# Five PSUM banks in one ring, output half columns in turns and merged VectorE work, in a fused forward and backward pass of an SSM and a gated FFN

## The chip, the core and the metric

The kernel runs on one core of a Trainium2 chip. A core has a matrix engine (TensorE, PE in the profile; its weight loads are PEld), a vector engine (VectorE, DVE), a scalar engine (ScalarE, ACT), GpSimd (POOL) and the queues that issue DMA (SP and others). Matmul results land in PSUM, which has eight banks; each holds 512 fp32 values per partition. VectorE or ScalarE must copy a result out of its bank before the bank is used again. SBUF is the memory for everything else on the core.

The metric is the device time of one execution, in microseconds (us). Of a kernel several executions are timed, and the median is given.

## The reference, cut to what matters

The input x (2048 rows of 576 columns, bf16) is normalised. The output is x plus a state-space convolution of xn (branch A) plus a gated FFN of xn (branch B). The program computes this output and, for a given grad_out, the gradients of x, of all parameters of A and of the three FFN matrices.

```python
def _B_ref(x, W_gate, W_up, W_down):            # D = 576, F = 4608
    gate = x @ W_gate
    up = x @ W_up
    gate = gate * (gate > 0)
    h = gate * up
    return h @ W_down

def _A_ref(u, A_re, A_im, B_re, B_im, C_re, C_im, log_dt, Dskip):
    dt = exp(log_dt)                            # per column d, N = 128 states
    P = exp(dt * A * l)                         # l = 0 .. 2047
    K = einsum("dn,dnl,dn->dl", C, P, dt * B).real
    y = causal_convolution(u, K)                # by rfft / irfft over 2 * L
    return y + u * Dskip

xn = layernorm(x)
out = x + _A_ref(xn, ...) + _B_ref(xn, ...)
# returned: out and the vjp of grad_out for x, A's eight parameters, W_gate, W_up, W_down
```

## The kernel before: the parts that matter

The FFN goes over the hidden size in 12 chunks (c) of 384 columns, each of three tiles (ft) of 128; the rows go in four segments (sg) of 512. The convolution (class S4) is cut into many small steps, which are interleaved with the FFN's by estimates of time; a scheduler orders the instructions of each engine.

PSUM is divided among three pools. Three banks hold FFN products and outputs, three belong to S4, and two to the FFN's transposes ("turns"):

```python
g.psum_mm = pool("psum_mm", 3, space=PSUM)
g.psum_s4 = pool("psum_s4", 3, space=PSUM)
g.psum_t = pool("psum_t", 2, space=PSUM)
```

A unit of the FFN makes gate, up and dh (the gradient of h) for 128 hidden columns and 512 rows: three groups of five matmuls of 512 columns (line L244). ScalarE applies relu, VectorE makes the masked up (upm), h and the two gradients; turns of earlier units are woven in, of which each is four 128x128 transposes and one copy:

```python
def a_unit(self, c, sg, ft, turns=()):
    ...
    for i, rhs in enumerate((xT, xT, gT)):
        ...
        ps = g.psum_mm.tile([P, 512], F32, name="ps_mm")
        for k in range(NK):
            nc.tensor.matmul(ps[:], lhsT=w[:, k, fs], rhs=rhs[:, k, :], ...)      # L244
        pss.append(ps)
        for _ in turns:
            next(src)
        yield ...
    ps_g, ps_u = pss[0:2]
    ...
    nc.scalar.activation(rg[:], ps_g[:], ACT.Relu)                                # L252
    nc.vector.scalar_tensor_tensor(upm[:], rg[:], 0.0, ps_u[:], op0=ALU.is_gt, op1=ALU.mult)   # L254
    nc.vector.tensor_tensor(hT[:], rg[:], upm[:], op=ALU.mult)                    # L256
    ...
    g.bal.copy(dhb, pss[2][:], 512)
    nc.vector.tensor_tensor(dgT[:], dhb, upm[:], op=ALU.mult)                     # L262
    nc.vector.tensor_tensor(duT[:], dhb, rg[:], op=ALU.mult)                      # L264
```

`bal.copy` gives a copy out of PSUM to VectorE or ScalarE by a running estimate of their loads (lines L62 and L68 in the profile).

An output step makes, for 128 rows, the two outputs (0: the FFN's output from h, three matmuls a group; 1: the gradient of xn from dg and du, six), each in two halves of 288 columns:

```python
def outdx(self, c, sg, j, last=None, turns=()):
    ...
    for which in range(2):
        for hf in range(2):
            ...
            ps = g.psum_mm.tile([P, 512], F32, name="ps_mm")
            for i, (lt, rh, cs) in enumerate(mms):
                nc.tensor.matmul(ps[:, cs], lhsT=lt, rhs=rh, ...)                 # L301
            if last is None:
                g.bal.copy(o[:, which, hs], ps[:, :DH], DH)
            ...
        if which == 0:
            yield FTC * 0.245
    ...
    yield FTC * 0.49
```

Its result is added to an accumulator in DRAM (osx to acc_dram). The last chunk instead adds S4's parts and finishes the outputs.

In S4, the products of two complex spectra (real and imaginary parts stacked on partitions, 96 such products):

```python
def product(self, pool, wpool, A, B, conj):
    ...
    v.tensor_tensor(t[:], A, B, op=ALU.mult)                                      # L666
    for i in range(2):
        r = slice(i * 64, (i + 1) * 64)
        v.tensor_tensor(Z[0:64, i, :], t[r, 0, :], t[r, 1, :], ...)               # L669
    v.tensor_tensor(t[:, 0, :], A[:, 0, :], B[:, 1, :], op=ALU.mult)              # L670
    v.tensor_tensor(t[:, 1, :], A[:, 1, :], B[:, 0, :], op=ALU.mult)              # L671
    for i in range(2):
        r = slice(i * 64, (i + 1) * 64)
        v.tensor_tensor(Z[64:P, i, :], t[r, 1, :], t[r, 0, :], ...)               # L674
    g.bal.add(d=1.6)
```

and, for each of 144 groups of four columns, the powers Y = A0 * B1 + V with V = A1 * B0 (L876 to L878, 1024 bf16 elements each), their use as weights of small matmuls (L903), their transposes (L913), and the sums that the parameter gradients need (matmuls L927):

```python
    for vi, r0 in enumerate((1, 0)):
        pr = gp.tile(sh, F32, name="pr")                                          # one buffer
        nc.vector.tensor_tensor(pr[:], X[...], psg[...], op=ALU.mult)             # L931
        nc.vector.tensor_reduce(out=Sm[:, vi, ...], in_=pr[:], op=ALU.add, axis=AX.X)   # L932
```

Of the kernel before, what the change touches and what calls it, by code (L numbers as in the profile page):

```python
# [10 lines left out]
F32 = mybir.dt.float32  # L11
# [67 lines left out]
def make_consts(g):  # L79
    nc, consts = g.nc, g.consts  # L80
    g.ident_bf = consts.tile([P, P], BF16, name="ident_bf")
    make_identity(nc, g.ident_bf[:])
    g.ident_f = consts.tile([P, P], F32, name="ident_f")
    make_identity(nc, g.ident_f[:])
# [14 lines left out]
def col_store(g, pool, psum, col, dst):  # L99

    nc = g.nc
    ps = psum()
    nc.tensor.transpose(out=ps[:NK, :P], in_=col, identity=g.ident_f[:])
# [14 lines left out]
def ln_group(g, pools, sg, x4, gT):  # L118
# [28 lines left out]
            nc.scalar.activation(x4[:, j, :], x4[:, j, :], ACT.Identity, bias=neg[:, j:j + 1])  # L147
    for j in range(JS):
        nc.vector.tensor_scalar(xn4[:, j, 0:D], x4[:, j, :], g.rinv[:, t0 + j:t0 + j + 1], None, op0=ALU.mult)
        pt = g.psum_t.tile([P, 8, P], BF16, name="pt")  # L150
        for k in range(NK):
            nc.tensor.transpose(out=pt[:, k, :], in_=xn4[:, j, k * P:(k + 1) * P], identity=g.ident_bf[:])
        (nc.vector.tensor_copy if j % 2 == 0 else nc.scalar.copy)(xT[:, :, j * P:(j + 1) * P], pt[:, 0:NK, :])  # L153
# [7 lines left out]
class Ffn:  # L161
# [68 lines left out]
    def a_unit(self, c, sg, ft, turns=()):  # L230

        g, nc = self.g, self.g.nc
        src = self.t_steps(turns)
        xT, gT = self.X[(c, sg)]
        fs = slice(ft * P, (ft + 1) * P)
        pss = []
        dhb = self.dh0.get(ft) if (c, sg) == (0, 0) else None
        for i, rhs in enumerate((xT, xT, gT)):
            if i == 2 and dhb is not None:
                continue  # L240
            w = self.wd[i]
# [9 lines left out]
        rg = self.ep.tile(shp, BF16, name="rg")  # L251
        nc.scalar.activation(rg[:], ps_g[:], ACT.Relu)  # L252
        upm = self.ep.tile(shp, BF16, name="upm")
        nc.vector.scalar_tensor_tensor(upm[:], rg[:], 0.0, ps_u[:], op0=ALU.is_gt, op1=ALU.mult)  # L254
        hT = self.tp.tile(shp, BF16, name="hT")
        nc.vector.tensor_tensor(hT[:], rg[:], upm[:], op=ALU.mult)  # L256
# [4 lines left out]
        dgT = self.tp.tile(shp, BF16, name="dgT")  # L261
        nc.vector.tensor_tensor(dgT[:], dhb, upm[:], op=ALU.mult)  # L262
        duT = self.tp.tile(shp, BF16, name="duT")
        nc.vector.tensor_tensor(duT[:], dhb, rg[:], op=ALU.mult)  # L264
        self.T[(c, sg, ft)] = (hT, dgT, duT)

    def t_steps(self, units):
        g, nc = self.g, self.g.nc
        for c, sg, ft in units:
            for src, dst in zip(self.T[(c, sg, ft)], (self.hN, self.dgN, self.duN)):  # L270
                pt = g.psum_t.tile([P, 8, P], BF16, name="pt")
                for j in range(JS):
                    nc.tensor.transpose(out=pt[:, j, :], in_=src[:, j * P:(j + 1) * P], identity=g.ident_bf[:])  # L273
                g.bal.copy(dst[:, sg * JS:(sg + 1) * JS, ft * P:(ft + 1) * P], pt[:, 0:JS, :], 512, fp32=False)
                yield

    def outdx(self, c, sg, j, last=None, turns=()):
# [7 lines left out]
            last.begin(t)  # L285
        src = self.t_steps(turns)
        Ts = [self.T[(c, sg, ft)] for ft in range(FTC)]
        for which in range(2):
            for hf in range(2):
                hs = slice(hf * DH, (hf + 1) * DH)  # L290
                if which == 0:
                    mms = [(Ts[ft][0], self.wf[:, 0, ft, hs]) for ft in range(FTC)]
# [11 lines left out]
                else:  # L304
                    last.take(t, which, hf, hs, ps[:, :DH])
                next(src, None)
            if which == 0:
                yield FTC * 0.245
        if last is not None:
            last.end(t)  # L310
        elif c == 0:
            nc.gpsimd.dma_start(g.acc_dram[:, t, :, :], o[:])
        else:
            nc.gpsimd.dma_start(g.acc_dram[:, t, :, :], o[:], accum_op=ALU.add)  # L314
        yield FTC * 0.49

    def rows(self, c, i):

# [144 lines left out]
class Ahead:  # L463
# [3 lines left out]
        self.load, self.total, self.n = load, total, n  # L467
        self.next, self.q = 0, {}

    def get(self, i):  # L470
        while self.next < min(i + self.n, self.total):
            self.q[self.next] = self.load(self.next)
            self.next += 1
        return self.q.pop(i)

class S4:
# [183 lines left out]
    def product(self, pool, wpool, A, B, conj):  # L660

        g, nc = self.g, self.g.nc
        t = wpool.tile([P, 2, DH], BF16, name="pr_t")
        Z = pool.tile([P, 2, DH], BF16, name="pr_z")
        v = nc.vector
        v.tensor_tensor(t[:], A, B, op=ALU.mult)  # L666
        for i in range(2):
            r = slice(i * 64, (i + 1) * 64)
            v.tensor_tensor(Z[0:64, i, :], t[r, 0, :], t[r, 1, :], op=ALU.add if conj else ALU.subtract)  # L669
        v.tensor_tensor(t[:, 0, :], A[:, 0, :], B[:, 1, :], op=ALU.mult)  # L670
        v.tensor_tensor(t[:, 1, :], A[:, 1, :], B[:, 0, :], op=ALU.mult)  # L671
        for i in range(2):
            r = slice(i * 64, (i + 1) * 64)
            v.tensor_tensor(Z[64:P, i, :], t[r, 1, :], t[r, 0, :], op=ALU.subtract if conj else ALU.add)  # L674
        g.bal.add(d=1.6)
        return Z


# [120 lines left out]
    def p2_pools(self, c):  # L799
# [2 lines left out]
        lv = cp.tile([P, ST], F32, name="lv")  # L802
        iota(nc, lv[:], [[1, ST]], 0, 16)
        return (lv,) + tuple(self.pool(c, n, bufs) for n, bufs in (
            ("k_par", 1), ("k_dk", 2), ("k_ex", 2), ("k_x", 1), ("k_xo", 2), ("k_uv", 1), ("k_yo", 3), ("k_yt", 2), ("k_g", 1)))

    def p2(self, hf, pools, pw):

        g, nc, bal = self.g, self.g.nc, self.g.bal
        v = nc.vector  # L810
        lv, parp, dkp, exp_, xp, xop, uvp, yop, ytp, gp = pools
        pend, turned = [], []
        Sm = parp.tile([P, 2, DH, 2], F32, name="Sm")

# [3 lines left out]
            return ex  # L818

        def load_dk(i):  # L820
            dkr = dkp.tile([P, ST, SC], BF16, name="dkr")
            nc.sync.dma_start(dkr[:].rearrange("p (q a) d -> p q a d", q=4), self.dk_dram[hf][:, :, i])
            return dkr
        exq, dkq = Ahead(load_ex, DH // SX, 2), Ahead(load_dk, DH // SC, 2)
        for gi in range(DH // SC):
            s0 = gi * SC
            dkr = dkq.get(gi)
# [3 lines left out]
            nc.gpsimd.tensor_tensor(dkc[:, :, 1, :], dkv, lv[:].unsqueeze(1).to_broadcast([P, SC, ST]), op=ALU.mult)  # L831
            Kst = dkp.tile([P, ST, SC], BF16, name="Kst")
            for x0 in range(0, SC, SX):
                hs = slice(hf * DH + s0 + x0, hf * DH + s0 + x0 + SX)
                ex = exq.get((s0 + x0) // SX)
                xs = [P, SX, NE]
# [31 lines left out]
                for dd in range(x0, x0 + SX, DG):  # L868
# [11 lines left out]
                    pend.append((Y, XC, X, dkc, Kst, Sm, s0, dd, dd - x0, hf, gi))  # L880
                    yield 2.1
                    if len(turned) > 0:
                        self.sums(turned.pop(0), gp)
                        yield 0.8
                    if len(pend) > 1:
                        yield from self.turn(pend.pop(0), ytp, turned)
        while pend or turned:
            if turned:
                self.sums(turned.pop(0), gp)
                yield 0.8  # L890
            if pend:
                yield from self.turn(pend.pop(0), ytp, turned)
# [23 lines left out]
        turned.append((YT, X, dkc, Sm, s0, dd, dx))  # L916
        yield 0.4

    def sums(self, item, gp):

        g, nc, bal = self.g, self.g.nc, self.g.bal
        YT, X, dkc, Sm, s0, dd, dx = item
# [5 lines left out]
        sh = [P, DG, 2, 32]  # L928
        for vi, r0 in enumerate((1, 0)):
            pr = gp.tile(sh, F32, name="pr")  # L930
            nc.vector.tensor_tensor(pr[:], X[:, dx:dx + DG, r0:r0 + 2].rearrange("p d r a -> p d (r a)").unsqueeze(2).to_broadcast(sh), psg[:, 0:DG * 64].rearrange("p (d j c) -> p d j c", j=2, c=32), op=ALU.mult)  # L931
            nc.vector.tensor_reduce(out=Sm[:, vi, s0 + dd:s0 + dd + DG, :], in_=pr[:], op=ALU.add, axis=AX.X)  # L932
        bal.add(d=1.3)

    def param_grads(self, hf, Sm, pw, xp, yop):

# [175 lines left out]
def kernel(  # L1112
# [30 lines left out]
    g.out_dskip = out_9  # L1143
    pool = lambda name, bufs, **kw: ctx.enter_context(tc.tile_pool(name=name, bufs=bufs, **kw))
    g.consts = pool("consts", 1)
    g.psum_mm = pool("psum_mm", 3, space=PSUM)
    g.psum_s4 = pool("psum_s4", 3, space=PSUM)
    g.psum_t = pool("psum_t", 2, space=PSUM)
    g.dram = pool("dram", 1, space=DRAM)
    make_consts(g)  # L1150
    d = lambda name, shape, dt=BF16: g.dram.tile(shape, dt, name=name)
# [100 lines left out]
```

## Time and profile before

Three runs of the kernel before took 1817.7 to 1819.48 us, the median is 1818.5 us. The profiled execution spans 1820.2 us.

| Engine | Busy, us | Share of the span | Instructions |
|---|---|---|---|
| PE (matmuls) | 1731.2 | 95% | 16303 |
| PEld (weight loads) | 1186.8 | 65% | 16449 |
| DVE (VectorE) | 1359.8 | 75% | 3181 |
| ACT (ScalarE) | 1184.4 | 65% | 2710 |
| POOL (GpSimd) | 205.0 | 11% | 246 |

A row of instruction groups gives line, engine, operation, result and operands, the shape and the count; then the busy time in us, the mean length of one in ns, and the idle time of the engine just before them with what ended it. For example:

```profile
L68 ACT CAST osx<-ps_mm 128x288 bf16<-128x288 f32 x675 | 262.2, 427 | 74.3 <-PE ps_mm L301 71.4
L254 DVE SCALAR_TENSOR_TENSOR upm<-rg,ps_mm 128x512 bf16<-128x512 bf16 x144 | 98.5, 684 | 92.6 <-PE ps_mm L244 70.7
L932 DVE TENSOR_REDUCE Sm<-pr 128x8 f32<-128x256 f32 x288 | 119.9, 416 | 3.6
```

Copies of output halves on ScalarE take 427 ns each; before them ScalarE stood idle for 74.3 us in all, of which 71.4 us ended when PE finished an output group. A row of waits gives who waited for whom, and then the total in us, how often, and the longest. A row of a timeline gives start and length in us, engine, line and work. The matmuls' ends are modelled, and some matmul records are missing from the trace (2000 of L244's 2145).

### The profile page before, as it was taken

The numbers are of one execution on the slowest core, as the hardware profiler recorded it, in microseconds if no ns is written. First come the engines' busy times: TensorE is split into PE (matmuls) and PEld (weight loads), VectorE is DVE, ScalarE is ACT, GpSimd is POOL, SyncE is SP. The second block draws the span as 40 slices with busy tenths as digits, with TensorE's granted clock in tenths as the row PEclk, the third lists the DMA queues.
The fourth block names the chain that finished last, engine by engine and source line by source line (L and its number), as shares of the span: only waits on it lengthen the run. The fifth ranks groups of instructions, "written<-read, shape, count | busy, mean of one in ns | idle before, by whom it ended". The sixth has DMA issues, their size and how long they took to land. (4 is left out here: it accounts for less than half of the span.)

```text
span 1820.2 us, 42157 instructions
## 1 busy us (share of the span) xinstructions
PE 1731.2 (95%) x16303; PEld 1186.8 (65%) x16449; DVE 1359.8 (75%) x3181; ACT 1184.4 (65%) x2710; POOL 205.0 (11%) x246
## 2 busy tenths in 40 slices
PE   7998998999999999999999999999999999999998
PEld 5664556668566666766756766766676675676776
DVE  7575886676888789669687889989979863983551
ACT  5874774686578478568468657747756845764551
POOL 0200012012012012011101101101111100110000
PEclk9999999999999999999999999999999999999999
DMA  8798999678568676776757856856675578995883
GB/s 288 261 323 307 286 263 292 188 189 231 177 132 199 179 185 136 222 193 153 216 159 175 237 159 136 213 178 159 155 198 137 94 219 248 267 291 152 264 250 96
DMA packets 239004, 373.30 MB, mean 205 GB/s; under 512 B 49490, under 2 KB 153428, under 8 KB 237268
## 3 DMA queue, kind: packets, MB, share of 16 engines
q1 hardware_dynamic: 212836, 304.09, 51.6%
q0 software_dynamic: 24384, 51.92, 18.9%
q10 hardware_dynamic: 1584, 14.60, 2.3%
q8 instruction: 128, 2.10, 0.5%
q14 instruction: 72, 0.59, 0.1%
HBM read 233.10 MB, written 137.43 MB: 204 GB/s over the span
## 5 line engine op out<-in xcount | busy, mean ns | idle before, releaser
L68 ACT CAST osx<-ps_mm 128x288 bf16<-128x288 f32 x675 | 262.2, 427 | 74.3 <-PE ps_mm L301 71.4
L314 POOL DMA_DIRECT2D acc_dram<-osx x160 | 138.5, 866 | 1073.0 <-ACT osx L68 718.8
L301 PE MATMUL ps_mm<-wf,dgT 128*128 128x288 bf16 x1152 | 208.6, 288 | 13.7 <-ACT osx L68 7.7
L355 PEld LDWEIGHTS <-rows 128*128 128x128 bf16 x1536 | 146.1, 98 | 96.7 <-issue 6.9
L301 PE MATMUL ps_mm<-wf,duT 128*128 128x288 bf16 x1152 | 206.9, 288 | 0.0
L301 PE MATMUL ps_mm<-wf,hT 128*128 128x288 bf16 x1152 | 185.2, 288 | 15.3 <-DVE upm L254 9.3
L244 PE MATMUL ps_mm<-gT,wd_160 128*128 128x512 bf16 x694 | 176.3, 381 | 6.3 <-ACT obd L68 4.4
L244 PE MATMUL ps_mm<-xT,wd_159 128*128 128x512 bf16 x711 | 178.4, 379 | 0.6 <-issue 0.2
L244 PE MATMUL ps_mm<-xT,wd_158 128*128 128x512 bf16 x595 | 168.9, 379 | 7.6 <-ACT xT L153 0.7
L254 DVE SCALAR_TENSOR_TENSOR upm<-rg,ps_mm 128x512 bf16<-128x512 bf16 x144 | 98.5, 684 | 92.6 <-PE ps_mm L244 70.7
L339 PE MATMUL ps_mm<-rows,hN 128*128 128x144 bf16 x2304 | 158.4, 226 | 0.0
L339 PEld LDWEIGHTS <-hN 128*128 128x128 bf16 x2304 | 147.4, 98 | 4.1 <-issue 1.4
L68 ACT CAST obw<-ps_mm 128x384 bf16<-128x384 f32 x104 | 49.5, 477 | 147.5 <-PE ps_mm L355 116.1
L301 PEld LDWEIGHTS <-dgT 128*128 128x128 bf16 x1152 | 107.7, 98 | 47.5 <-issue 21.9
L355 PE MATMUL ps_mm<-dgN,rows 128*128 128x384 bf16 x768 | 137.4, 328 | 0.6 <-ACT rg L252 0.6
L355 PE MATMUL ps_mm<-duN,rows 128*128 128x384 bf16 x768 | 136.6, 326 | 0.6 <-DVE upm L254 0.5
L301 PEld LDWEIGHTS <-hT 128*128 128x128 bf16 x1152 | 104.8, 98 | 44.8 <-issue 15.5
L301 PEld LDWEIGHTS <-duT 128*128 128x128 bf16 x1152 | 113.3, 99 | 29.8
L252 ACT ACTIVATE rg<-ps_mm 128x512 bf16<-128x512 f32 x144 | 87.2, 606 | 55.1 <-PE ps_mm L244 52.9
L932 DVE TENSOR_REDUCE Sm<-pr 128x8 f32<-128x256 f32 x288 | 119.9, 416 | 3.6
L68 ACT CAST dhb<-ps_mm 128x512 bf16<-128x512 f32 x141 | 84.0, 595 | 56.9 <-PE ps_mm L244 54.8
L244 PEld LDWEIGHTS <-wd_159 128*128 128x128 bf16 x720 | 65.3, 98 | 61.9 <-issue 1.5
(2517 smaller groups left out, 3534.1 us busy)
## 6 DMA issues: line engine op xcount, KB each, us to landing
acc_dram<-osx POOLq DMA_DIRECT2D x176, 288.0 KB, 4.9
gT<-in_gT_dram SPq DMA_DIRECT2D x48, 640.0 KB, 6.3
xT<-xT_dram SPq DMA_DIRECT2D x44, 640.0 KB, 6.1
rows<-in_gq_dram SPq DMA_DIRECT2D x48, 576.0 KB, 4.6
wf<-in_Wf_dram ACTq DMA_DIRECT2D x11, 1296.0 KB, 9.3
ex_dram<-exs SPq DMA_DIRECT2D x36, 320.0 KB, 4.0
ex<-ex_dram SPq DMA_DIRECT2D x36, 320.0 KB, 4.3
out_dram<-obw SPq DMA_DIRECT2D x96, 96.0 KB, 2.5
```

Source lines behind the costliest of these rows:

```text
L68: self.nc.scalar.copy(out, in_)
L244: nc.tensor.matmul(ps[:], lhsT=w[:, k, fs], rhs=rhs[:, k, :], start=(k == 0), stop=(k == NK - 1))
L252: nc.scalar.activation(rg[:], ps_g[:], ACT.Relu)
L254: nc.vector.scalar_tensor_tensor(upm[:], rg[:], 0.0, ps_u[:], op0=ALU.is_gt, op1=ALU.mult)
L301: nc.tensor.matmul(ps[:, cs], lhsT=lt, rhs=rh, start=(i == 0), stop=(i == len(mms) - 1))
L314: nc.gpsimd.dma_start(g.acc_dram[:, t, :, :], o[:], accum_op=ALU.add)
L339: nc.tensor.matmul(ps[:, ft * 144:(ft + 1) * 144], lhsT=self.hN[:, st, ft * P:(ft + 1) * P], rhs=gq[:, st, :], start=(st == 0), stop=(st = ...
L355: nc.tensor.matmul(ps[:, :Fc], lhsT=xs[:, st, 0:P], rhs=src[:, st, :], start=(st == 0), stop=(st == ST - 1))
L932: nc.vector.tensor_reduce(out=Sm[:, vi, s0 + dd:s0 + dd + DG, :], in_=pr[:], op=ALU.add, axis=AX.X)
```

## The change

It has five parts.

1. The five banks of FFN products and turns become one ring of five.
2. An output step goes through its groups half by half: output 0 and output 1 of the first half, then both of the second, instead of both halves of output 0 first. The points at which S4's steps may come in move along with it.
3. The two FFN gradients are one VectorE instruction over 1024 elements, with dh read twice; h and the gradients lie in one tile.
4. The two products of the sums go into one buffer (that of V) and one reduction takes both. In the products of spectra, the two cross products get a tile of their own (w), the multiplications come first, and the four additions are ordered so that less changes in partitions from one to the next.
5. To make room, the fp32 identity and the pool of pr go, and dkr has one buffer instead of two, loaded ahead in the middle of a group.

It is for letting PE run further ahead of the engines that empty its banks, and for less VectorE work per unit.

```diff
-    g.psum_mm = pool("psum_mm", 3, space=PSUM)
+    g.psum_mm = pool("psum_mm", 5, space=PSUM)
     g.psum_s4 = pool("psum_s4", 3, space=PSUM)
-    g.psum_t = pool("psum_t", 2, space=PSUM)
...
-                pt = g.psum_t.tile([P, 8, P], BF16, name="pt")
+                pt = g.psum_mm.tile([P, 512], F32, name="ps_mm")[:].bitcast(BF16).rearrange("p (k t) -> p k t", t=P)
... (the same for the turns of the normalised input)
-        for which in range(2):
-            for hf in range(2):
+        for hf in range(2):
+            for which in range(2):
...
-            if which == 0:
-                yield FTC * 0.245
+            if hf == 0:
+                yield FTC * 0.3675
...
-        yield FTC * 0.49
+        yield FTC * 0.3675
... (a_unit)
+        ru = self.ep.tile([P, 2, JS * P], BF16, name="rg")
+        upm, rg = ru[:, 0], ru[:, 1]
...
+        T = self.tp.tile([P, 3, JS * P], BF16, name="T")
+        nc.vector.tensor_tensor(T[:, 0], rg, upm, op=ALU.mult)
...
-        nc.vector.tensor_tensor(dgT[:], dhb, upm[:], op=ALU.mult)
-        nc.vector.tensor_tensor(duT[:], dhb, rg[:], op=ALU.mult)
+        nc.vector.tensor_tensor(T[:, 1:3], dhb.unsqueeze(1).to_broadcast([P, 2, JS * P]), ru[:], op=ALU.mult)
... (product)
+        w = wpool.tile([P, 2, DH], BF16, name="pr_w")
         v.tensor_tensor(t[:], A, B, op=ALU.mult)
...
+            v.tensor_tensor(w[:, i, :], A[:, i, :], B[:, 1 - i, :], op=ALU.mult)
+        top, low = slice(0, 64), slice(64, P)
+        re = lambda i, r: v.tensor_tensor(Z[0:64, i, :], t[r, 0, :], t[r, 1, :], ...)
+        im = lambda i, r: v.tensor_tensor(Z[64:P, i, :], w[r, 1, :], w[r, 0, :], ...)
+        re(0, top)
+        im(0, top)
+        im(1, low)
+        re(1, low)
+        g.bal.add(d=2.0)
... (dkr)
-            dkr = dkp.tile([P, ST, SC], BF16, name="dkr")
+            dkr = drp.tile([P, ST, SC], BF16, name="dkr")
...
+                if x0 > 0 and gi + 1 < DH // SC:
+                    dkq.ahead(gi + 1)
... (sums)
+        pr = uvp.tile([P, DG, 2, P], BF16, name="V")[:]. ... .bitcast(F32). ...
         for vi, r0 in enumerate((1, 0)):
-            pr = gp.tile(sh, F32, name="pr")
-            nc.vector.tensor_tensor(pr[:], X[...], psg[...], op=ALU.mult)
-            nc.vector.tensor_reduce(out=Sm[:, vi, ...], in_=pr[:], op=ALU.add, axis=AX.X)
-        bal.add(d=1.3)
+            nc.vector.tensor_tensor(pr[:, vi], X[...], psg[...], op=ALU.mult)
+        nc.vector.tensor_reduce(out=Sm[:, :, ...], in_=pr..., op=ALU.add, axis=AX.X)
+        bal.add(d=1.35)
```

More of the change, by code (lines that the diff above doesn't have):

```diff
@@ L82, in make_consts @@
     make_identity(nc, g.ident_bf[:])
-    g.ident_f = consts.tile([P, P], F32, name="ident_f")
-    make_identity(nc, g.ident_f[:])
     g.hpcol = consts.tile([P, 1], F32, name="hpcol")
@@ L102, in col_store @@
     ps = psum()
-    nc.tensor.transpose(out=ps[:NK, :P], in_=col, identity=g.ident_f[:])
+    ident = pool.tile([P, JS * P], BF16, name="rg")[:, 0:2 * P].bitcast(F32)
+    make_identity(nc, ident)
+    nc.tensor.transpose(out=ps[:NK, :P], in_=col, identity=ident)
     row = pool.tile([P, JS * P], BF16, name="dhb")[0:NK, 0:P]
@@ L250, in a_unit @@
         shp = [P, JS * P]
[L251 to L256, printed above, removed]
+        ru = self.ep.tile([P, 2, JS * P], BF16, name="rg")
+        upm, rg = ru[:, 0], ru[:, 1]
+        nc.scalar.activation(rg, ps_g[:], ACT.Relu)
+        nc.vector.scalar_tensor_tensor(upm, rg, 0.0, ps_u[:], op0=ALU.is_gt, op1=ALU.mult)
+        T = self.tp.tile([P, 3, JS * P], BF16, name="T")
+        nc.vector.tensor_tensor(T[:, 0], rg, upm, op=ALU.mult)
         g.bal.add(d=1.6, a=0.48)
@@ L260, in a_unit @@
             g.bal.copy(dhb, pss[2][:], 512)
-        dgT = self.tp.tile(shp, BF16, name="dgT")
-        nc.vector.tensor_tensor(dgT[:], dhb, upm[:], op=ALU.mult)
-        duT = self.tp.tile(shp, BF16, name="duT")
-        nc.vector.tensor_tensor(duT[:], dhb, rg[:], op=ALU.mult)
-        self.T[(c, sg, ft)] = (hT, dgT, duT)
+        nc.vector.tensor_tensor(T[:, 1:3], dhb.unsqueeze(1).to_broadcast([P, 2, JS * P]), ru[:], op=ALU.mult)
+        self.T[(c, sg, ft)] = tuple(T[:, i] for i in range(3))
     def t_steps(self, units):
@@ L270, in t_steps @@
             for src, dst in zip(self.T[(c, sg, ft)], (self.hN, self.dgN, self.duN)):
-                pt = g.psum_t.tile([P, 8, P], BF16, name="pt")
+                pt = g.psum_mm.tile([P, 512], F32, name="ps_mm")[:].bitcast(BF16).rearrange("p (k t) -> p k t", t=P)
                 for j in range(JS):
@@ L468, in __init__, with ahead @@
         self.next, self.q = 0, {}
-    def get(self, i):
+    def ahead(self, i):
         while self.next < min(i + self.n, self.total):
@@ L473, in get @@
             self.next += 1
+    def get(self, i):
+        self.ahead(i)
         return self.q.pop(i)
@@ L667, in product @@
         for i in range(2):
[L668 to L675, printed above, removed]
+            v.tensor_tensor(w[:, i, :], A[:, i, :], B[:, 1 - i, :], op=ALU.mult)
+        top, low = slice(0, 64), slice(64, P)
+        re = lambda i, r: v.tensor_tensor(Z[0:64, i, :], t[r, 0, :], t[r, 1, :], op=ALU.add if conj else ALU.subtract)
+        im = lambda i, r: v.tensor_tensor(Z[64:P, i, :], w[r, 1, :], w[r, 0, :], op=ALU.subtract if conj else ALU.add)
+        re(0, top)
[3 more added lines that the diff above has]
+        g.bal.add(d=2.0)
         return Z
@@ L804, in p2_pools @@
         return (lv,) + tuple(self.pool(c, n, bufs) for n, bufs in (
-            ("k_par", 1), ("k_dk", 2), ("k_ex", 2), ("k_x", 1), ("k_xo", 2), ("k_uv", 1), ("k_yo", 3), ("k_yt", 2), ("k_g", 1)))
+            ("k_par", 1), ("k_dr", 1), ("k_dk", 2), ("k_ex", 2), ("k_x", 1), ("k_xo", 2), ("k_uv", 1), ("k_yo", 3), ("k_yt", 2)))
     def p2(self, hf, pools, pw):
@@ L810, in p2 @@
         v = nc.vector
-        lv, parp, dkp, exp_, xp, xop, uvp, yop, ytp, gp = pools
+        lv, parp, drp, dkp, exp_, xp, xop, uvp, yop, ytp = pools
         pend, turned = [], []
@@ L820, in load_dk @@
         def load_dk(i):
-            dkr = dkp.tile([P, ST, SC], BF16, name="dkr")
+            dkr = drp.tile([P, ST, SC], BF16, name="dkr")
             nc.sync.dma_start(dkr[:].rearrange("p (q a) d -> p q a d", q=4), self.dk_dram[hf][:, :, i])
             return dkr
-        exq, dkq = Ahead(load_ex, DH // SX, 2), Ahead(load_dk, DH // SC, 2)
+        exq, dkq = Ahead(load_ex, DH // SX, 2), Ahead(load_dk, DH // SC, 1)
         for gi in range(DH // SC):
@@ L882, in p2 @@
                     if len(turned) > 0:
-                        self.sums(turned.pop(0), gp)
+                        self.sums(turned.pop(0), uvp)
                         yield 0.8
@@ L888, in p2 @@
             if turned:
-                self.sums(turned.pop(0), gp)
+                self.sums(turned.pop(0), uvp)
                 yield 0.8
@@ L917, in turn, with sums @@
         yield 0.4
-    def sums(self, item, gp):
+    def sums(self, item, uvp):
         g, nc, bal = self.g, self.g.nc, self.g.bal
@@ L928, in sums @@
         sh = [P, DG, 2, 32]
+        pr = uvp.tile([P, DG, 2, P], BF16, name="V")[:].rearrange("p d r q -> p (d r q)").bitcast(F32).rearrange("p (v d j c) -> p v d j c", v=2, d=DG, j=2)
         for vi, r0 in enumerate((1, 0)):
-            pr = gp.tile(sh, F32, name="pr")
-            nc.vector.tensor_tensor(pr[:], X[:, dx:dx + DG, r0:r0 + 2].rearrange("p d r a -> p d (r a)").unsqueeze(2).to_broadcast(sh), psg[:, 0:DG * 64].rearrange("p (d j c) -> p d j c", j=2, c=32), op=ALU.mult)
-            nc.vector.tensor_reduce(out=Sm[:, vi, s0 + dd:s0 + dd + DG, :], in_=pr[:], op=ALU.add, axis=AX.X)
-        bal.add(d=1.3)
+            nc.vector.tensor_tensor(pr[:, vi], X[:, dx:dx + DG, r0:r0 + 2].rearrange("p d r a -> p d (r a)").unsqueeze(2).to_broadcast(sh), psg[:, 0:DG * 64].rearrange("p (d j c) -> p d j c", j=2, c=32), op=ALU.mult)
+        nc.vector.tensor_reduce(out=Sm[:, :, s0 + dd:s0 + dd + DG, :].rearrange("p v d j -> p v (d j)"), in_=pr.rearrange("p v d j c -> p v (d j) c"), op=ALU.add, axis=AX.X)
+        bal.add(d=1.35)
     def param_grads(self, hf, Sm, pw, xp, yop):
```

## The prediction

> **What bounds the kernel now.** I read the shares of busy time first, then the row of 40 slices, the chain that ended last, the waits of PE, and at last the timeline of one output step.
>
> ```profile
> PE 1731.2 (95%) x16303; PEld 1186.8 (65%) x16449; DVE 1359.8 (75%) x3181; ACT 1184.4 (65%) x2710; POOL 205.0 (11%) x246
> ...
> PE   7998998999999999999999999999999999999998
> ...
> PEclk9999999999999999999999999999999999999999
> ```
>
> PE is busy from end to end, and the clock is granted in full nearly always (mean 0.99). So a gain can only come from PE working without holes. How large are they? 1820.2 - 1731.2 = 89 us by the busy row, but that row flatters: a 288-column matmul is shown as 286 ns long although the next one starts 0.12 us later, so a hole shorter than the 0.17 us of overlap is not seen. I therefore took the distance from each matmul's start to the next one's. The stretch after the last output step shows what PE does unhindered (start, length, work, count):
>
> ```profile
> 1779.95 12.00 PE ps_mm L339 x192
> 1791.95 20.80 PE ps_mm L355 x128
> ```
>
> 12.00/192 = 62.5 ns for 144 columns, 20.80/128 = 162.5 ns for 384: about 0.42 ns a column. Charging every matmul of the trace its columns leaves these holes in front of the matmuls of each line, in us: outputs (L301) 61, products (L244) 18 (49 less 31 for 145 records that the trace lacks, at 0.216 each), small S4 matmuls of 16 and 32 columns (L903, L927) 47, turns (L273) 15, S4's first transform (L628) 13, weight gradients (L355, L339) 16, S4's transposes (L913) 8. Of the 47 some 38 are no wait at all: such a matmul takes about 27 ns whatever its columns. Of the rest the outputs are the big item, 61 us in 192 steps, or 0.32 us a step. Who ends them:
>
> ```profile
> PE ps_mm L301 <- DVE upm L254: 10.4, 12, 3.4
> ...
> PE ps_mm L301 <- ACT osx L68: 7.7, 11, 1.7
> ...
> PE ps_mm L301 <- DVE hT L256: 3.8, 3, 1.9
> PE ps_mm L301 <- ACT dhb L68: 3.4, 8, 1.0
> PE ps_mm L301 <- ACT rg L252: 1.8, 2, 1.1
> ```
>
> Total, times, longest, in us. Counted from start to start the same causes are larger: ACT osx 16, DVE upm 13, ACT dhb 6, DVE hT 4.5, ACT rg 2. All but hT are the emptying of a bank of the three of ps_mm. One step shows how (start, length, engine, work):
>
> ```profile
> 805.11 1.00 ACT L845 ACTIVATE W<-xa,hpcol 128x640 f32<-128x640 f32 x1
> ...
> 805.45 0.53 PE L301 MATMUL ps_mm<-wf,dgT 128*128 128x288 bf16 x3
> ...
> 805.82 0.53 PE L301 MATMUL ps_mm<-wf,duT 128*128 128x288 bf16 x3
> 805.84 1.17 ACT L68 CAST osx<-ps_mm 128x288 bf16<-128x288 f32 x3
> ...
> 806.45 0.53 PE L301 MATMUL ps_mm<-wf,dgT 128*128 128x288 bf16 x3
> ```
>
> The three duT matmuls from 805.82 need 0.37 us, so the next could start at 806.19. It starts at 806.45, as ACT was held by an S4 sine until 806.11 and the bank came free only then. ACT in the mean is not late (65%), it is late in bursts, and three banks don't carry PE over a burst of 1 us.
>
> **What the Trainium skill says.** "Perfetto Trace Analysis", Optimizing Tensor Performance (Matmuls), tells to rotate independent groups through different banks so that emptying one overlaps the next group; its Optimization Strategy section takes a gap that repeats as a sign of too few buffers. The step above agrees, 0.26 us. "VectorE: DVE Perf Modes", on two Vector instructions with no wait between them, states that an instruction whose first input or output starts in another quadrant of partitions than the last one's is held until all earlier ones have finished. This trace agrees: in the product, two additions on different halves (L669) start 0.312 us apart with 0.299 of length, while two whole-width multiplications (L670, L671) start 0.226 apart with 0.307. The same page's tier table gives a bf16 tensor_tensor two elements a cycle and tensor_reduce one. The trace agrees: 1024 bf16 elements in 0.69 us, 512 in 0.42, and 256 reduced in 0.416.
>
> **The change part by part.**
>
> *Banks.* FFN has five banks before and after (three for products, two for turns); now they are one ring. In a stretch of outputs without turns, PE may run five groups ahead in place of three. A group lasts 0.37 or 0.74 us, so the slack grows from about 1.1-1.6 us to 2.2-2.7. Bursts like the one shown (1.0 us of sine, 1.2 of copies) then fit. In a unit with turns the ring mixes: product, turn, turn, product... The fifth allocation back is then often the product of up, which is held until VectorE's upm has run, so a turn may now wait for upm where it waited only for its own copies. Expected of the 37 us of bank waits in front of L301: two thirds go, 25 us. Of the product's waits on obd at the start of a unit (4.7, start to start) nearly all, 4. Of L273, 2, net of new waits.
>
> *Half columns in turns.* Before, the four groups are 3, 3, 6, 6 matmuls; after, 3, 6, 3, 6. A copy takes 0.427 us, a 3-group 0.37, a 6-group 0.74: two short ones in a row outran one emptying engine by 0.12 us. The matmuls are the same number, and so are the copies. It helps the banks, and is worth little alone: up to 0.06 us in each of 192 steps, counted in the 25.
>
> *FFN gradients merged.* dgT and duT start 0.335 us apart each: 0.67 for both. One tensor_tensor of 1024 bf16 elements starts 0.602 after the one before (the row Y). 0.068 x 144 = 10 us of VectorE.
>
> *Sums.* Two products stay; two reductions of 256 become one of 512: 2 x 0.33 against 0.60, 0.06 saved. Chains in which each waits for the one in front (0.455 in place of 0.33) occurred 155 times in 144 groups; perhaps half go: 0.06 more. About 0.12 x 144 = 17 us. But the products now lie in V's only buffer: the next V can't run ahead of a reduction that waits for PE. I take back 5.
>
> *Products.* Seven instructions before and after. Before, six of seven start held (from the end of the one in front to the start +13 to +35 ns, in place of -84); with the order top/top, top/low, low/low, low/top and a separate w, four are: 2 x 0.11 x 96 = 21 us.
>
> VectorE in all: 10 + 12 + 21 = 43 of 1360 us, 3%. It isn't the bound, so this pays only where PE waits for it: upm (in the 25), hT 4.5, and S4's waits for pr and pr_z, some 10 together. I give 4 for it.
>
> *The rest.* The estimates by which copies go to VectorE or ScalarE rise a little (product 1.6 to 2.0, sums 1.3 to 1.35): osx on ScalarE 675 to 682, s_ug 117 to 125. About 12 copies more of 0.43 us, 5 us of ScalarE. One dkr buffer less, asked for half a group earlier: S4's groups last some 65 us (18 of them between 315 and 1494 us), a load under 10. S4's place among the FFN work stays the same within 0.1% of the matmul order.
>
> Sum: 25 + 4 + 2 + 4 = 35 us. Work removed from one wait comes back in part as another, as PE then presses harder on the same two engines, which are at 87% of VectorE and 68% of ScalarE between 900 and 1200 us (260.3 and 205.2 of 300). I take a quarter off in the stages that lie in such company, and keep nothing at the end: from 1620 us on holes in front of outputs are 2 us in all. 35 - 6 = 29, and 1818.5 - 29, rounded, is **1789 us**.
>
> **The rivals.**
>
> 1. *The ring turns into a new wait.* For it: PE waited up to 3.4 us for an upm that came late in VectorE's order, and turns now share banks with the product that upm empties. In that case L273 waits for upm, the gain shrinks to some 5 us: 1813.
> 2. *ScalarE is the bound in the output stages.* For each segment (3 units, 15 turns, 16 output groups) it has 3 x 1.2 + 15 x 0.60 + 16 x 0.427 = 19.4 us, against PE's 3 x 3.2 + 15 x 0.21 + 4 x 2.2 = 21.6, before S4's copies. More banks can't help a mean that is short. Against it: ScalarE still sat idle for PE 71 us before osx and 55 before dhb. It would give 10 us: 1808.
> 3. *VectorE matters more than I grant it.* S4 and FFN share it at 87%; if many short holes behind it vanish too, most of the 100 us that are not inherent halve: 1770.
> 4. *V as the buffer of sums stalls S4's chain* and VectorE's queue with it: each of 144 groups may lose 0.1-0.2 us of VectorE: the VectorE gain is gone, 1795.
>
> **Range and chances.** 8 in 10 between **1768 and 1810**. Two per cent faster is 1782, 7 us below my number, within reach of rival 3: **0.36**. Within 2%: **0.61**. Slower by 2% (1855) needs a new serial wait in every unit: **0.03**.
>
> **What would show it.** Right: holes in front of L301 (start to start) fall from 61 to 30-36 us and ACT osx and dhb nearly leave PE's waits; VectorE's busy time falls to 1300-1325 us; one 1024-element row of 0.69 us replaces dgT and duT; the reduction of 512 takes 0.68. Rival 1 shows as PE's turns waiting for the upm instruction (now named rg, on L254); rival 2 as the L301 waits staying on ACT with more ScalarE busy per segment; rival 4 as V waiting for PE's L927 by way of the reduction. The prediction is wrong if the holes in front of L301 shrink and the span doesn't, for then they come back elsewhere.

## The result, and the profile after

The changed kernel takes 1805.8 us in the median of four runs (1801.6 to 1809.7), the kernel before 1818.1 us on the same chip. The ratio is 0.9931, with a 95% interval of 0.9907 to 0.9955: 0.7% faster, 12 us. The prediction was 1789, 29 us. So the change does what it is for, and more than half of the gain is missing.

The first row of the page after the change (busy us, share of the span, instructions):

```profile
span 1808.0 us, 41947 instructions
...
PE 1714.8 (95%) x16303; PEld 1186.7 (66%) x16449; DVE 1310.2 (72%) x2867; ACT 1187.5 (66%) x2736; POOL 204.3 (11%) x246
```

VectorE has 50 us less to do, ScalarE 3 more, and PE is still busy from end to end. PE's own waits (total, times, longest; the output matmuls are L298 now, the turns L270, upm is written into rg on L254):

```profile
PE ps_mm L270 <- DVE T L256: 4.3, 4, 1.6
...
PE ps_mm L298 <- DVE T L256: 2.5, 3, 1.1
PE ps_s_9335 L917 <- DVE V L935: 2.3, 1, 2.3
PE ps_mm L298 <- DVE rg L254: 2.2, 4, 1.0
```

In front of the outputs ScalarE's osx (7.7 us before) is gone, dhb fell from 3.4 to 0.4, and upm from 10.4 to 2.2. What is left there is mostly data that isn't ready (T on L256 is h). So half of the hole that the change aims at has closed. A new line has come up: S4's transposes (L917, in the kernel before L913) wait for VectorE's product of the sums (L935, written into V). Counted per group of instructions (busy us, mean ns, then the idle time in front and who ended it):

```profile
L298 PE MATMUL ps_mm<-wf,T 128*128 128x288 bf16 x3456 | 484.0, 288 | 7.2 <-DVE T L256 2.5 <-DVE rg L254 2.2 <-DVE osx L62 0.9
...
L936 DVE TENSOR_REDUCE Sm<-V 128x16 f32<-128x512 f32 x144 | 98.4, 683 | 1.8
L261 DVE TENSOR_TENSOR T<-dhb,rg 128x1024 bf16<-128x1024 bf16 x141 | 98.2, 697 | 26.6 <-ACT dhb L68 26.5
...
L917 PEld LDWEIGHTS <-Y 128*128 128x128 bf16 x1152 | 68.8, 97 | 18.2 <-DVE V L935 12.8 <-issue 1.5
```

The merged instructions cost what was expected (0.697 and 0.683 us). The last line is the news: 12.8 us of S4's weight loads waiting for L935; in the kernel before the same weight loads waited 1.3 us for that product.

The same accounting as in the prediction (from each matmul's start to the next one's, less its columns) shows the exchange. For this and for all the kernels below, holes in us, from the one profiled execution of each; S4 is the sum over its seven kinds of matmul groups. About 38 us of it are no wait, since the short matmuls take longer than their columns; nor are some 8 us of the outputs', where a matmul of 288 columns takes 122 ns and is charged 120. Both are the same in every row. With one trace for a kernel, a difference of a few us between two rows may be chance.

| Kernel | Banks FFN, turns, S4 | Ratio to before, 95% | Outputs | S4 | VectorE busy |
|---|---|---|---|---|---|
| before | 3, 2, 3 | 1 | 61 | 76 | 1360 |
| changed | ring of 5, 3 | 0.9931 (0.9907-0.9955) | 30 | 98 | 1310 |
| a_ring | ring of 5, 3 | 0.9941 (0.9925-0.9957) | 36 | 93 | 1359 |
| b_ring_half | ring of 5, 3 | 0.9922 (0.9910-0.9933) | 38 | 89 | 1357 |
| c_sums_old | ring of 5, 3 | 0.9899 (0.9884-0.9914) | 35 | 91 | 1329 |
| d_pr_bf16 | ring of 5, 3 | 0.9916 (0.9904-0.9929) | 32 | 91 | 1313 |
| e_vec_only | 3, 2, 3 | 1.0012 (1.0004-1.0021) | 55 | 81 | 1312 |
| f_split | 3, 2, 3 | 0.9981 (0.9971-0.9990) | 48 | 88 | 1310 |
| i_c_4_4 | ring of 4, 4 | 0.9863 (0.9849-0.9877) | 40 | 59 | 1330 |
| k_after_4_4 | ring of 4, 4 | **0.9836** (0.9821-0.9851) | 39 | 59 | 1310 |
| l_before_4_4 | ring of 4, 4 | 0.9915 (0.9894-0.9936) | 46 | 67 | 1357 |
| n_b_4_4 | ring of 4, 4 | 0.9876 (0.9861-0.9891) | 44 | 63 | 1356 |
| m_c_3_5 | ring of 3, 5 | 1.0047 (1.0033-1.0061) | 43 | 63 | 1329 |
| j_c_ring8 | one ring of 8 | 0.9945 (0.9933-0.9958) | 30 | 69 | 1330 |

From before to changed: outputs -31, S4 +22, all others -3; together -12, which is the difference of the spans. It is the sign of being wrong that the prediction names at its end: the holes in front of the outputs shrink, and the span shrinks by much less. The rest of this text is about the 22.

### The profile page after: what moved, and what is told of

Read it like the earlier page. It is cut to its first block, busy times and chain, and to the rows that moved or that the text cites. A ratio compares the mean times of both kernels' runs of the same rounds, so it can differ in the third digit from the quotient of the medians.

```text
span 1808.0 us, 41947 instructions
## 1 busy us (share of the span) xinstructions
PE 1714.8 (95%) x16303; PEld 1186.7 (66%) x16449; DVE 1310.2 (72%) x2867; ACT 1187.5 (66%) x2736; POOL 204.3 (11%) x246
## 5 line engine op out<-in xcount | busy, mean ns | idle before, releaser
L298 PE MATMUL ps_mm<-wf,T 128*128 128x288 bf16 x3456 | 484.0, 288 | 7.2 <-DVE T L256 2.5
L298 PEld LDWEIGHTS <-T 128*128 128x128 bf16 x3456 | 324.8, 98 | 94.1 <-issue 10.6
L254 DVE SCALAR_TENSOR_TENSOR rg<-rg,ps_mm 128x512 bf16<-128x512 bf16 x144 | 98.6, 685 | 119.7 <-PE ps_mm L244 91.1
L270 PEld LDWEIGHTS <-T 128*128 128x128 bf16 x1728 | 127.4, 98 | 88.1 <-DVE T L256 7.1
L244 PE MATMUL ps_mm<-xT,wd_151 128*128 128x512 bf16 x711 | 178.9, 379 | 0.6 <-issue 0.2
L244 PE MATMUL ps_mm<-xT,wd_150 128*128 128x512 bf16 x595 | 164.5, 379 | 11.6 <-ACT xT L153 1.6
L270 PE MATMUL ps_mm<-ident_bf,T 128*128 128x128 bf16 x1728 | 157.7, 220 | 7.9 <-DVE T L256 4.3
L261 DVE TENSOR_TENSOR T<-dhb,rg 128x1024 bf16<-128x1024 bf16 x141 | 98.2, 697 | 26.6 <-ACT dhb L68 26.5
L244 PEld LDWEIGHTS <-wd_150 128*128 128x128 bf16 x720 | 66.3, 98 | 64.9 <-issue 5.2
L244 PEld LDWEIGHTS <-wd_151 128*128 128x128 bf16 x720 | 65.0, 98 | 60.1 <-issue 2.1
L244 PEld LDWEIGHTS <-wd_152 128*128 128x128 bf16 x705 | 63.3, 98 | 57.8 <-issue 1.2
```

The costliest lines, as they stand in the source:

```text
L254: nc.vector.scalar_tensor_tensor(upm, rg, 0.0, ps_u[:], op0=ALU.is_gt, op1=ALU.mult)
L261: nc.vector.tensor_tensor(T[:, 1:3], dhb.unsqueeze(1).to_broadcast([P, 2, JS * P]), ru[:], op=ALU.mult)
L298: nc.tensor.matmul(ps[:, cs], lhsT=lt, rhs=rh, start=(i == 0), stop=(i == len(mms) - 1))
```

## Experiments: which part costs, and is it the tie of the sums to V?

Theory T, formed from the L917 line: pr now lies in V's only buffer, so the sums wait for their turn behind V, hold S4's banks longer, and PE waits. Rival R: the fault is not in the sums; PE, freed in the outputs, only presses harder on the same two engines.

**c_sums_old**: the changed kernel with the sums as before.

```diff
-        nc.vector.tensor_reduce(out=Sm[:, :, ...], in_=pr..., op=ALU.add, axis=AX.X)    # one, pr in V
+            pr = gp.tile(sh, F32, name="pr")                                             # own buffer, two reductions
+            nc.vector.tensor_reduce(out=Sm[:, vi, ...], in_=pr[:], op=ALU.add, axis=AX.X)
```

> The changed kernel with the sums as they were (pr in a buffer of its own, two products and two reductions of 256). Theory T (pr in V's only buffer ties the sums to the order of the V products, S4's banks are held longer, and PE waits in front of S4's transposes): holes in front of the transposes fall from 19 to 8-10 us, those of the 16-column matmuls from 32 to 28, VectorE has 9-17 us more work, and the time falls from 1806 to 1790-1796. Rival R (PE only presses harder on the same two engines, so what the ring wins comes back in front of S4 whatever the sums do): time within 4 us of the changed kernel, 1802-1810, the holes stay.

Measured 1802.8 us, 0.9899, which is R's range: better than the changed kernel by perhaps 0.3%, with intervals that still overlap. The holes in front of the transposes fell from 19 to 11 us and those of the 16-column matmuls from 32 to 27, about as T says. But other kinds rose (the first transform from 17 to 20), and S4 in all fell only from 98 to 91. So T explains 7 of the 22 us at most.

**f_split**: the changed kernel with three and two banks.

```diff
-    g.psum_mm = pool("psum_mm", 5, space=PSUM)
+    g.psum_mm = pool("psum_mm", 3, space=PSUM)
+    g.psum_t = pool("psum_t", 2, space=PSUM)
```

> The changed kernel with the banks split again, three and two. T: holes in front of the outputs rise from 30 to 45-60 us, S4's holes stay at their new size, since the sums are still tied to V: 1820-1830, no better than the kernel before. R: with the outputs slow again the pressure goes, S4's holes return to those of before: 1815-1819.

Measured 0.9981, 1816, in R's range. The outputs' holes are 48, as T says. S4's are 88: they neither stayed at 98 nor went back to 76. So each theory has a share in the holes.

**a_ring**: the kernel before with the ring of five alone.

> The kernel before with the ring of five banks alone. T: holes in front of the outputs 30-38 us and S4's as before: 1788-1796, better than the whole change. R: S4's holes grow by as much as in the changed kernel: 1803-1810.

Measured 0.9941, 1809. The outputs' holes fell from 61 to 36, as the step in the prediction says, and S4's rose from 76 to 93 without any change of the sums. This is R's figure, and it takes T down as the main cause: of the 22 us that were given back, 17 come with the ring alone.

**e_vec_only**: the merged VectorE work alone. The kernel keeps part 5 of the change too (one buffer for dkr); in its trace PE waits 0.8 us in all for what is made from dkr.

> The merged VectorE work alone (sums in V's buffer, FFN gradients, products), banks split and halves in the old order. T: VectorE's busy time falls by 45-50 us and yet the time rises, by the 10-20 us in front of S4: 1822-1835. R: VectorE's relief is worth a little: 1810-1818.

Measured 1.0012 (1.0004 to 1.0021), 1822: 48 us less of VectorE work, and no gain; 2 us lost. It lies at the edge of T's range, with S4's holes up by 5 us only, not by 10 to 20; the outputs' fell by 6, and those of the turns rose by 3.

**b_ring_half**: ring and halves, no merged VectorE work.

> The kernel before with the ring of five and the half columns in turns, none of the VectorE work merged. If the parts add up (the ring alone 10.7 us, the halves some 5 by the split-bank run), 1800-1804, as good as or better than the whole change; holes in front of the outputs 26-30 us, down from 36 with the ring alone. If the halves only do again what the ring does: 1806-1810.

Measured 0.9922, 1804, in the range of adding up, but not for the reason given: the outputs' holes should have fallen to 26-30 us and are 38 (36 with the ring alone). The step over the ring alone (3.5 us) is within the intervals. This kernel is as fast as the whole change: with three banks for S4 the VectorE work merged is worth nothing that can be seen.

**d_pr_bf16**: the changed kernel with the merged sums in a buffer of their own; the products are rounded to bf16, to save room.

```diff
-        pr = uvp.tile([P, DG, 2, P], BF16, name="V")...
+        pr = gp.tile([P, 2, DG, 2, 32], BF16, name="pr")[:]
```

> The changed kernel, sums merged into one reduction, but the two products in a buffer of their own, kept in bf16 so that it fits (the products of the sums are rounded to bf16). The same instructions as the changed kernel; only the tie to V is gone. Tie (theory T): PE's holes in front of S4's transposes fall from 19 to 9-12 us, and the time to 1798-1803. If instead the merged reduction itself is what costs (one longer instruction, later result): stays at 1804-1808.

The time, 1802.5, is in T's range, but T's reason isn't there. The weight loads of the transposes wait for the product as before:

```profile
L917 PEld LDWEIGHTS <-Y 128*128 128x128 bf16 x1152 | 68.8, 97 | 17.0 <-DVE pr L935 12.0 <-issue 1.0
```

12.0 us with its own buffer, 12.8 in V's. T's mechanism is refuted: it is not the buffer that makes PE wait for the product. What happens is to be seen in the changed kernel's timeline, at its longest wait for L935 (start, length, engine, work):

```profile
578.67 0.35 PE L931 MATMUL ps_s_9294<-dkc,YT 128*128 128x32 bf16 x8
...
579.32 0.69 DVE L861 TENSOR_TENSOR X<-W,ex 128x512 f32<-128x512 f32 x1
...
580.04 0.69 DVE L868 TENSOR_TENSOR W<-pw,X 128x512 f32<-128x512 f32 x1
...
580.10 0.35 PE L907 MATMUL ps_s_9325<-XC,Y 128*128 128x16 bf16 x8
...
580.65 0.69 DVE L867 TENSOR_TENSOR xa<-pw,X 128x512 f32<-128x512 f32 x1
...
581.37 0.69 DVE L869 TENSOR_TENSOR XC<-xa,W 128x512 bf16<-128x512 f32 x1
...
581.80 0.44 ACT L68 CAST fC_9321<-ps_s_9322 128x288 bf16<-128x288 f32 x1
581.98 0.74 DVE L935 TENSOR_TENSOR V<-X,ps_s_9294 128x256 f32<-128x256 f32 x2
582.10 0.27 ACT L68 CAST Kst<-ps_s_9325 128x64 bf16<-128x64 f32 x1
...
582.78 0.62 PE L917 MATMUL ps_s_9335<-ident_bf,Y 128*128 128x128 bf16 x8 [2.33 <-DVE V L935]
```

The sums' matmuls are done by 579.0. VectorE has four fp32 instructions in front of the product in its queue, so the bank of ps_s_9294 is freed at 582.7. S4 has two banks besides: ps_s_9322 and ps_s_9325 take them at 579.97 and 580.10. ScalarE, with five copies of osx in front of it until 581.94, empties these two only at 582.24 and 582.37. The transposes need a fourth bank and stand for 2.33 us, and the FFN's matmuls behind them in PE's queue stand too, though the FFN's banks have been emptied by 581.94.

## Experiments: the division of the banks

Theory C: S4's three banks are now the short ones; a bank is worth more there than as the FFN's fifth. There are eight, so it can be tried by shifting one.

```diff
-    g.psum_mm = pool("psum_mm", 5, space=PSUM)
-    g.psum_s4 = pool("psum_s4", 3, space=PSUM)
+    g.psum_mm = pool("psum_mm", 4, space=PSUM)
+    g.psum_s4 = pool("psum_s4", 4, space=PSUM)
```

**i_c_4_4**: c_sums_old with four and four.

> The changed kernel with the old sums, and with four banks for the FFN and four for S4 instead of five and three. Theory C (what the ring won came back in front of S4's groups because S4's three banks now are the short ones): S4's holes (first transform, transposes, sums, mixes) fall by 8-15 us, those of the outputs rise by 5-8: 1797-1802. Rival (VectorE and ScalarE, not the banks, set S4's pace): outputs lose, S4 wins nothing: 1805-1812.

Measured 0.9863, 1792, faster than C's range: S4's holes fell by 32 us (91 to 59), the outputs' rose by 5.

**k_after_4_4**: the changed kernel with four and four, nothing else altered.

> The changed kernel, nothing else altered, with four banks for the FFN's ring and four for S4. Theory C (five and three starve S4, so what the outputs win is given back in front of S4's groups): holes in front of S4's transposes fall from 19 to 7-12 us and the first transform's from 17 to 11-14, outputs rise from 30 to 38-42, time 1790-1796. Rival (the old sums were needed for it): 1800-1806.

Measured 1788.3 us, 0.9836: 30 us faster than before, the fastest of all, and a little faster than C's range. The outputs' holes (39) and the transposes' (7.5) are as C says, the first transform's (10) are smaller. From PE's waits in it:

```profile
PE ps_mm L298 <- DVE rg L254: 6.2, 6, 1.8
...
PE ps_mm L298 <- ACT osx L68: 1.9, 3, 1.4
PE ps_s L917 <- ACT fC L68: 1.8, 3, 1.3
```

The wait of L917 for L935 is gone from the list (L917 now waits 1.8 us for fC, another of S4's copies), and a little of upm and osx has come back. The place of the timeline shown above, in this kernel:

```profile
571.31 0.36 PE L931 MATMUL ps_s<-dkc,YT 128*128 128x32 bf16 x8
...
573.43 0.90 PE L298 MATMUL ps_mm<-wf,T 128*128 128x288 bf16 x6 [1.39 <-ACT osx L68]
...
574.29 0.36 PE L907 MATMUL ps_s<-XC,Y 128*128 128x16 bf16 x8
...
574.49 0.61 PE L917 MATMUL ps_s<-ident_bf,Y 128*128 128x128 bf16 x8
574.62 0.75 DVE L935 TENSOR_TENSOR V<-X,ps_s 128x256 f32<-128x256 f32 x2
```

The product is as late as it was: 3.31 us from the start of its matmuls to its own, in both kernels. Yet the transposes start in front of it. A late product costs nothing here once there is a fourth bank. The exchange has its price at this very place too: PE now stands for 1.39 us in front of an output, as ScalarE's copies of osx are late for four banks. It is 1.39 us in place of 2.33.

Is it the number of banks, or do the instructions merely come in another order? Of the 16303 matmuls 15923 stand in the same order in the two kernels' traces, and of the 2867 VectorE instructions 2835. The stretch of S4 and FFN together, 320 to 1500 us, in the changed kernel and then in this one (length, busy us of PE, PEld, DVE, ACT, POOL with counts, clock, DMA share, GB/s):

```profile
320.00:1500.00 1180.00, 1140.25 (x11506) 797.83 (x11606) 945.95 (x1936) 804.69 (x1818) 154.16 (x164) 1.00 0.69 180
```

```profile
320.00:1500.00 1180.00, 1149.23 (x11595) 803.44 (x11694) 946.33 (x1939) 813.43 (x1844) 154.77 (x164) 1.00 0.70 183
```

In the same time PE gets 89 more matmuls done and is busy 9 us longer, while VectorE is busy for 946 us in both.

**l_before_4_4** and **n_b_4_4**: the kernel before with four and four, without and with the halves in turns, VectorE's work unmerged in both.

> The kernel before with one ring of four for FFN products and turns and four banks for S4, one bank less for the FFN than it had. Theory C: the ring needs only four banks to do better than three and two, and S4 is glad of the fourth: 1796-1803, below the ring of five (0.9941 of before). Rival (five are needed for the FFN, and four do only with halves in turns): 1808-1816.

> The kernel before with four and four banks and half columns in turns, and none of the VectorE work merged (VectorE busy 1357 us in place of 1310). If VectorE's relief is worth what I granted it (4 us and some in the waits for upm): 1795-1800 against 1792 with FFN gradients and products merged. If it is worth nothing: 1790-1793. If VectorE is the engine that sets the pace of S4's stretch: 1805 or more.

l: 0.9915, 1803, at the upper end of C's range: one bank fewer for the FFN than before the change, and still faster than before. It is not told apart from the ring of five (0.9941) by the intervals. n: 0.9876, in the range in which VectorE's relief is worth something: with four and four, merging all of VectorE's work (k) gives 0.4% over n, and the intervals don't touch. Halves in turns give as much here (l to n), with intervals that don't touch either.

**m_c_3_5**: the other side, three for the FFN and five for S4.

> The changed kernel with the old sums, three banks for the FFN and five for S4. Theory C has an optimum in the middle: outputs' holes 60-80 us, S4's as low as with four, so 1805-1825. If S4's banks are what matters above all: 1788-1794.

Measured 1.0047, 1826, just above C's range. S4's holes are about as with four (63, and 59 in i_c_4_4), so a fifth bank is of no use there. The FFN lost, though not where I looked: outputs 43, products 72 (48 in c_sums_old, in both traces with the same gap of missing records), turns 22.

```profile
PE ps_mm L270 <- DVE rg L254: 6.9, 10, 1.4
PE ps_mm L244 <- DVE rg L254: 5.8, 7, 1.9
```

With three banks the turns and the next products do wait for upm: it is the prediction's first rival, two banks further down.

**j_c_ring8**: all eight banks in one ring.

```diff
-        return self.g.psum_s4.tile([P, 512], F32, name="ps_s4")
+        return self.g.psum_mm.tile([P, 512], F32, name="ps_mm")
```

> The changed kernel with the old sums and all eight banks in one ring for FFN and S4. Theory C: both kinds of holes shrink, 1790-1798. Rival (one slow S4 group, held by VectorE for microseconds, now blocks the whole ring): holes in front of the FFN's groups return, 1805-1825.

Measured 0.9945, 1807: the time is in the rival's range, but not for its reason. The holes are small on both sides (30 and 69). It lost 12 us before the first chunk's weight gradients began (at 134.5 us, in the kernel before at 122.2), where the setup of S4 waits for ScalarE's sines (d_o) and an FFN product for a copy of the normalised input (xT):

```profile
PE ps_mm L555 <- ACT d_o L458: 13.1, 3, 9.2
...
PE ps_mm L244 <- ACT xT L153: 6.4, 1, 6.4
```

From there to the end it gained 28 us on the kernel before, in the one trace of each. So one ring for all did well here once all its users flowed. Why the start waits so was not followed up.

## Why the prediction was wrong, point by point

- *What bounds the kernel.* Right: PE's holes, and the largest in front of the outputs.
- *Banks and halves, 25 us in front of the outputs.* Right, a little more: 61 to 30 us. osx and dhb nearly left PE's waits. The ring alone did 25 of it. The 4 us in front of products came as 3; the 2 of the turns didn't come (15 to 16 us).
- *The halves, worth little alone.* Too low: with banks split they gave 0.3% (e to f), with four and four 0.4% (l to n), and only with the ring of five less than the measurement can tell.
- *VectorE's 43 us.* Right, a little more: 1360 to 1310. FFN gradients and products came as 31 (1360 to 1329 in c_sums_old), as predicted, the sums as 19 in place of 12. The product's additions behave as the prediction's rule on held instructions says. In the changed kernel's timeline:

```profile
631.70 0.30 DVE L669 TENSOR_TENSOR pr_w<-s_ug 128x288 bf16<-128x288 bf16 x1
631.92 0.29 DVE L671 TENSOR_TENSOR pr_z<-pr_t 64x288 bf16<-64x288 bf16 x1
632.23 0.62 DVE L672 TENSOR_TENSOR pr_z<-pr_w 64x288 bf16<-64x288 bf16 x2
632.86 0.30 DVE L671 TENSOR_TENSOR pr_z<-pr_t 64x288 bf16<-64x288 bf16 x1
```

  The first addition follows the multiplication freely (start to start 0.22); the next three start 0.31 to 0.32 apart, held.
- *4 us of time for it.* Not so with three banks for S4: e_vec_only lost 2. With four and four it was worth 7 (n to k, in which part 5 differs too).
- *The sum: "I take a quarter off", 6 us.* **This is the step that failed.** Of the 31 us won in front of the outputs, 22 came back in front of S4's groups. The text names the two engines as what PE would press on. It is S4's three banks: with one bank more (after to k) the 22 us vanish and 17 besides, while VectorE's busy time stays the same within 0.1 us. I had listed 68 of S4's 76 us of holes, had taken 38 of them as inherent, and never asked who ends the others.
- *Rivals.* 1, the ring as a new wait for upm: not at five, where upm ended 1.0 us of the turns' waits; at three it came. 2, ScalarE as the bound: no, its busy time rose by 3 us and the outputs' waits on it nearly left. 3, VectorE worth more: not with three banks for S4; with four, 7 us in place of 4, far from what the rival needs. 4, V as buffer of the sums: its sign, V held up by the reduction, is not there; VectorE stood idle for 1.2 us in all in front of V (L881), and 1.5 us in the kernel before. PE's wait for L935, 12.8 us, is another one, and stays with another buffer (d_pr_bf16).
- *Two slips in the working.* Rival 2 reckons with 15 turns in every segment of rows. There are 432 turns in 48 segments, so 9 in the mean, and its sum becomes 15.8 us of ScalarE against 20.3 of PE: ScalarE was further from being the bound than the text says. And a small matmul takes about 26 ns in a row, not 27.

What stays open: with three S4 banks, merged sums go with larger holes in front of the transposes (19 and 18 us with the ring of five, against 10 to 12 with the old sums). A later product is not the reason. From the last of the sums' matmuls to the product VectorE takes 1.1 us in the mean with either form (the changed kernel and c_sums_old), and the merged form gives the bank back sooner, 2.0 us after the first of these matmuls in place of 3.0. What differs is the bank that the transposes get. The place of the first timeline in c_sums_old, where the sums' matmuls start at 580.42:

```profile
583.05 0.61 PE L917 MATMUL ps_s<-ident_bf,Y 128*128 128x128 bf16 x8
...
583.99 0.41 DVE L935 TENSOR_TENSOR pr<-X,ps_s 128x256 f32<-128x256 f32 x1
```

Here too S4 has three banks and the same two groups came between, but the transposes don't wait for the sums' bank; they start 0.05 us after ScalarE has emptied fC's. So a pool's banks are not given out strictly in turn. In 55 of the 144 groups another S4 group than that of L907 stands between the sums and the transposes. With merged sums the transposes start within 0.1 us of the release of the sums' bank in 15 of these (changed kernel; 13.6 us of holes) and 14 (d_pr_bf16; 13.0); with the old sums in 6 (c_sums_old; 3.6), and in 30 they start while that bank is still held (4 in the changed kernel). Why the banks are given out in another way with merged sums was not tested.

## What to carry to other kernels

When a program's stages share the banks of PSUM, and PE takes their matmuls in one order, the shortest pool can stop all of them: before giving banks to the stage with the largest holes, ask what the other stage does with the ones it has, and try the divisions on both sides. Here 5 and 3 gave 0.7% and 4 and 4 gave 1.6% with the same code; with the old sums 5 and 3 gave 1.0%, 4 and 4 gave 1.4%, and 3 and 5 lost 0.5%. And a relief of an engine that isn't the bound may show its worth only when the buffers between it and the bound are enough: 48 us less of VectorE work gained nothing with S4's three banks (e_vec_only), and 46 us less gained 7 us with four (n to k).

## What the runs showed that I had not expected

- What a bank is worth depends on how many there are: the outputs' holes went from 30 with five banks to 39 with four, while S4's went from 98 with three to 59 with four. With the old sums S4's went from 91 with three to 59 with four, and 63 with five.
- What one VectorE instruction's dependence on the one in front costs: in the changed kernel h (L256) starts 0.72 us (median) after upm (L254), which it reads and which is 0.69 long; another instruction right after L254 starts 0.60 after it.
